# Reordering the first batch of a fused attention and feed-forward kernel: earlier loads of the second batch, and score bursts of 384 columns

## The chip, the cores and the metric

The kernel runs on one core of a Trainium2 chip. The metric is the device time of one execution in microseconds (us). The kernel before took 431.75 us (median of three runs, 431.38 to 431.86).

## What is computed

The reference is grouped-query attention followed by a feed-forward layer with a squared ReLU, over 8 batches (b0 to b7) of 384 tokens:

```python
scores = scale * np.matmul(q, k.transpose(0, 1, 3, 2))   # q: 8 x 16 heads x 384 x 64, k and v: 8 x 4 kv heads, each serving 4 heads
attn = exp(scores - max);  attn = attn / sum(attn)
x = matmul(attn, v).transpose(0, 2, 1, 3).reshape(3072, 1024)
h = np.maximum(x @ w_in, 0.0)        # w_in: 1024 x 2048
out = (h * h) @ w_out                # w_out: 2048 x 1024
```

Inputs and output are f32; the kernel computes in bf16 with f32 accumulation and leaves out the subtraction of the maximum.

## The kernel before, in words

**Work of a batch.** The 384 tokens are three blocks of 128. A batch has four kv groups (g0 to g3) of four heads, and 12 units: one kv group with one block of keys. The scores of a unit are 128 keys by 1536 columns (4 heads x 384 queries), held as two halves x=0,1 of 768 columns (two heads each, stacked on partitions 0-63 and 64-127 of `qT`). ScalarE (ACT) takes `exp` of them from PSUM into `expT`. A "pair" c (two per kv group) is the product of the exponentials with the values, 18 matmuls with 65 columns in function `av`; its last column is the softmax sum, by which VectorE (DVE) divides (`rinv`, `o_sb`). The result is turned into `xT` (in b0 on TensorE, `turn_o_pe`; later by a transposing DMA, `turn_o_dma`). The feed-forward part of a batch is 128 "up" matmuls (line 426: 16 column blocks of 8) and 96 "down" matmuls (line 471: six outputs of 16), with relu on DVE (434), square on ACT (436), output copies on DVE (480) and stores on SP (483).

**Keys and queries must be turned** before scores: keys are doubled into `k_dup`, then keys and queries are turned into `kT` and `qT`. For b0 and b1 TensorE does it (`turn_k_pe`, three transposes; `turn_q_pe`, six) with a DVE copy after each; from b2 on SP issues transposing DMAs (lines 266 and 272).

**Order of the work.** The kernel is written as a list. `Recorder.add` appends an operation to its engine's list, with the tiles that it reads and writes, and works out a modelled end from a `cost`; `emit` gives each engine its list in that order with the semaphore waits that follow. So the order on every engine is fixed when the program is built. TensorE's order is chosen by the loop at lines 575 to 675: at each step it collects what could come next (a turn, a pair, a turn of the output, a score burst, a piece of the feed-forward) with the modelled time at which its inputs are there, and takes among those that are ready the one with the lowest priority number: score bursts of b0 are 0, turns 1, pairs 2, output turns 3, later score bursts 4, feed-forward 5.

**Scores of b0** come in small bursts (`burst_small`, list `smalls`), of 1024 values per partition each: a whole unit's columns 0 to 511, and after each second unit the columns 512 to 767 of two units together. That is 18 bursts and 18 `exp` instructions at line 337. A burst takes two of PSUM banks 0 to 3 alternately; turns and pairs share banks 4 and 5 while b0's bursts last, and the feed-forward has banks 6 and 7. Batches b1 to b7 use `burst_two` (lines 347 and 357): two units, six banks, 3072 values per partition.

**Loads.** The queue of GpSimd (POOL) carries nearly all loads, with a cast from f32. After b0's own loads and three key copies, it issues w_in pieces 0 to 2 (512 KB each), then keys (192 KB), queries (two of 384 KB) and values of b1, then w_in pieces 3 to 7, then the key copy `k_dup` and value copy `v_aug` of b1, four pieces of w_out (1024 KB each), and then keys, queries and values of b2. The first keys and queries of b0 come uncast over the SP and ACT queues: `q_f32` in one transfer, cast by DVE (columns 0 to 511 of 768) and by ACT (columns 512 to 767). The queries of g0 are turned in two steps: tiles 0 to 3, then tiles 4 and 5.

Of the kernel before, what the change touches and what calls it, by code (L numbers as in the profile page):

```python
# [133 lines left out]
def bass_gqa_attention__then__ffn_squared_relu_kernel(  # L134
# [72 lines left out]
    def first_loads():  # L207

        def keys(eng, g0, g1):
            R.add(eng, lambda e: e.dma_start(  # L210
                k_f32[:, g0 * NJ:g1 * NJ, :].rearrange("p (g j) d -> p g (j d)", j=NJ),
                k[0, g0:g1].rearrange("g (p j) d -> p g (j d)", j=NJ)),
                writes=[("k_f32", g) for g in range(g0, g1)], dma=f"kf{g0}", cost=0.4 * (g1 - g0), issue=0.4)

        keys("sync", 0, 1)
        R.add("scalar", lambda e: e.dma_start(
            q_f32[:, :, :], q[0, 0:4].rearrange("h (p j) d -> p h (j d)", j=NJ)),
            writes=["q_f32"], dma="qf", cost=1.3, issue=0.4)
        keys("scalar", 1, HKV)
# [8 lines left out]
    def load_q(b, h0, h1):  # L228
        st = b % NST
        R.add("gpsimd", lambda g: g.dma_start(  # L230
            q_st[st][:, h0:h1, :],
            q[b, h0:h1].rearrange("h (p j) d -> p h (j d)", j=NJ)),
            writes=[("q_st", st, h // 4, x) for h in range(h0, h1, 4) for x in range(2)], dma=f"q{st}_{h0}",
            cost=0.33 * (h1 - h0), issue=0.8)
# [36 lines left out]
    def turn_q_dma(b, half):  # L271
        R.add("sync", lambda e: e.dma_start_transpose(
            out=qT[b % 2][:, 12 * half:12 * half + 12, :],
            in_=q_st[b % NST][:, 8 * half:8 * half + 8, :].rearrange("p h e -> p (h e)")),
            reads=[("q_st", b % NST, 2 * half + i, x) for i in range(2) for x in range(2)],
            writes=[("qT", b % 2, 2 * half + i, x) for i in range(2) for x in range(2)], dma=f"turn_q{half}", cost=2.5)

# [15 lines left out]
    def turn_q_pe(b, g, banks, t0=0, t1=6):  # L293
        i = pick(banks)
        pt = bank(i).bitcast(bf16)
        src = q_st[b % NST][:, 4 * g:4 * g + 4, :].rearrange("p h e -> p (h e)")
        parts = [h for h in range(2) if t0 < (4, 6)[h] and t1 > (0, 4)[h]]

        def tr(pe):
            for t in range(t0, t1):  # L300
                m = pe.matmul(pt[:, (t - t0) * 128:(t - t0 + 1) * 128], src[:, t * 128:(t + 1) * 128], ident[:],  # L301
                              is_transpose=True)
            return m

        R.add("tensor", tr, reads=[("q_st", b % NST, g, h) for h in parts] + ["ident"], writes=[("bank", i)],
              cost=0.06 * (t1 - t0))
        dst = qT[b % 2][:, 6 * g + t0:6 * g + t1, :].rearrange("p n c -> p (n c)")
        R.add("vector", lambda e: e.tensor_copy(dst, pt[:, 0:(t1 - t0) * 128]),  # L308
              reads=[("bank", i)], writes=[("qT", b % 2, g, h) for h in parts], cost=0.07 + 0.068 * (t1 - t0))


    def score_reads(b, u, parts=(0, 1)):
        g = u // NJ
        return [("kT", b % 2, g)] + [("qT", b % 2, g, h) for h in parts]

# [4 lines left out]
    def burst_small(b, pieces, base):  # L320

        wide = 512 // len(pieces)

        def sc(pe):
            for n, (u, c0) in enumerate(pieces):
                for x in range(2):
                    m = pe.matmul(ps[:, base + x, n * wide:(n + 1) * wide],  # L327
                                  kT[b % 2][64 * x:64 * x + 64, u, :], q_cols(b, u // NJ, x, c0, c0 + wide))
            return m

        keys = [("bank", base), ("bank", base + 1)]
        R.add("tensor", sc, reads=[r for u, c0 in pieces for r in score_reads(b, u, (c0 // 512,))], writes=keys,
              cost=0.22 + 0.19)
        n, c0 = (b * NU + pieces[0][0]) % NEX, pieces[0][1]
        src = ps[:, base:base + 2, :].rearrange("p x (k c) -> p x k c", k=len(pieces))
        dst = expT[:, n:n + len(pieces), :, c0:c0 + wide].rearrange("p k x c -> p x k c")
        R.add("scalar", lambda e: e.activation(dst, src, AF.Exp, scale=0.125),  # L337
              reads=keys, writes=[("expT", (n + m) % NEX, c0 // 512) for m in range(len(pieces))], cost=0.92)

    def burst_two(b, u):  # L340

        def sc(pe):
            for k0, cols in ((0, ((0, 512), (512, 768))), (1, ((0, 256), (256, 768)))):
# [13 lines left out]
        R.add("scalar", lambda e: e.activation(dst, src, AF.Exp, scale=0.125),  # L357
              reads=keys, writes=[("expT", (n + m) % NEX, h) for m in range(2) for h in range(2)], cost=2.63)

    def av_reads(b, g):  # L360
        return [("expT", (b * NU + g * NJ + j) % NEX, h) for j in range(NJ) for h in range(2)] + [("v_aug", b % 2), ("v_one", b % 2)]

    def av(b, c, banks):
# [11 lines left out]

        R.add("tensor", lambda pe: mm(pe, 6 * s2), reads=av_reads(b, g), writes=[("bank", i)], cost=0.285)
        yield
        R.add("tensor", lambda pe: mm(pe, 6 * s2 + 3), reads=av_reads(b, g), writes=[("bank", i)], cost=0.285)
        r = (b * 8 + c) % 2
# [125 lines left out]
    aug_v(0, "gpsimd")  # L505
    for i in range(3):
        load_w_in(i)
    load_k(1)
    load_q(1, 0, 8)
    load_q(1, 8, 16)  # L510
    load_v(1)
    for i in range(3, 8):
        load_w_in(i)
    dup_k(1, "gpsimd")
    aug_v(1, "gpsimd")
# [7 lines left out]
    def warm_up(pe):  # L523
        for _ in range(14):
# [6 lines left out]
    q_from = q_f32.ap().rearrange("p h e -> p (h e)")  # L531
    R.add("vector", lambda e: e.tensor_copy(q_to[:, 0:512], q_from[:, 0:512]),
          reads=["q_f32"], writes=[("q_st", 0, 0, 0)], cost=0.6)
    R.add("scalar", lambda e: e.copy(q_to[:, 512:768], q_from[:, 512:768]),
          reads=["q_f32"], writes=[("q_st", 0, 0, 1)], cost=0.4)

# [3 lines left out]
    for u in range(NU):  # L540
        smalls.append([(u, 0)])
        if u % 2 == 1:
            smalls.append([(u - 1, 512), (u, 512)])
    turn_q = [(0, 0, "k"), (0, 0, "a"), (0, 0, "c")]
# [4 lines left out]
    turned_g = set()  # L549
    units, halves, pairs, turned, up_done = 0, set(), 0, 1, -1  # L550
    x_done = {b: 0 for b in range(B)}
# [16 lines left out]
    def open_bank(banks):  # L568
        return min(R.when(writes=[("bank", i)]) for i in banks)
# [5 lines left out]
    while av_q or av_open or sc_q or o_q or f_head is not None:  # L575
# [3 lines left out]
        if loaded + 1 < B and turned >= loaded and not turn_q:  # L579
# [5 lines left out]
            load_v(loaded)  # L585
        if not chores and queued < loaded and units >= queued * NU and pairs >= queued * 8:
            queued += 1
            prepare(queued)
# [5 lines left out]
        if turn_q:  # L594
            b, g, w = turn_q[0]
            src = [("k_dup", b, g)] if w == "k" else [("q_st", b, g, h) for h in range(2) if w != "ac"[1 - h]]
            cand.append((max(R.when(reads=src), open_bank(spare)), 1, "turn"))
        if av_open is not None:
            cand.append((now, 2, "av2"))
        elif av_q:  # L600
            b, c = av_q[0]
            if units >= b * NU + (c // 2 + 1) * NJ and up_done >= b - NXT:
                cand.append((max(R.when(reads=av_reads(b, c // 2)), open_bank(spare)), 2, "av"))
        if o_q:
            cand.append((max(R.when(reads=o_q[0][2]), open_bank(spare)), 3, "o"))
        if sc_q:
            b, u = sc_q[0]
            if b == 0:
                top = max(p[0] for p in smalls[u])
                ok = all((0, p[0] // NJ, p[1] // 512) in turned_g for p in smalls[u])  # L610
                ok = ok and pairs // 2 * NJ + NEX >= top + 1
                reads = [r for p in smalls[u] for r in score_reads(0, p[0], (p[1] // 512,))]
                t = max(R.when(reads=reads), R.when(writes=[("bank", 2 * (u % 2) + i) for i in range(2)]))
                if ok:
                    cand.append((t, 0, "sc"))
            else:
                ok = ((b, (u + 1) // NJ, 1) in turned_g) if b == 1 else turned >= b
                t = max(R.when(reads=score_reads(b, u) + score_reads(b, u + 1)),
# [17 lines left out]
        if what[2] == "turn":  # L636
            b, g, w = turn_q.pop(0)
            if w == "k":
                turn_k_pe(b, g, spare)
            else:  # L640
                turn_q_pe(b, g, spare, *dict(q=(0, 6), a=(0, 4), c=(4, 6))[w])
            turned_g |= {(b, g, h) for h in range(2) if w in ("q", "ac"[h])}
        elif what[2] == "av":
# [17 lines left out]
        elif what[2] == "sc":  # L661
            b, u = sc_q.pop(0)
            if b == 0:
                burst_small(0, smalls[u], 2 * (u % 2))
                halves |= {(p[0], p[1] // 512) for p in smalls[u]}
                while (units, 0) in halves and (units, 1) in halves:
                    units += 1
            else:
                burst_two(b, u)
                units += 2  # L670
        else:
# [34 lines left out]
```

The softmax here doesn't subtract the row's maximum and nothing guards it: scores larger than these inputs give would overflow.

## Time and profile before

| | us |
|---|---|
| median of three runs | 431.75 |
| span of the profiled execution | 430.6 |
| TensorE busy | 421.8 |
| ScalarE busy | 194.0 |
| VectorE busy | 158.9 |
| GpSimd busy | 55.6 |
| up matmuls, 1024 at line 426 | 174.5 |
| down matmuls at line 471 | 167.7 |
| `exp` of b0, 18 at line 337 | 16.9 |
| `exp` of b1 to b7, 42 at line 357 | 114.5 |

A row of the timeline gives the start, the length of a merged run of equal instructions, the engine, the line, output and inputs, the shape and the count; a bracket at its end gives the idle time of the engine before it and what ended that idle time. Matmul ends are modelled, so rows that overlap by a few tenths are one uninterrupted stream.

### The profile page before, as it was taken

Reading aid. Unit: us, or ns where it says so; the run is one execution under the profiler, and the core shown is the slowest. Engines: PE = TensorE matmul, PEld = TensorE weight load, DVE = VectorE, ACT = ScalarE, POOL = GpSimd, SP = SyncE. Lnnn points to the kernel's source line nnn. Section 1 sums busy time; section 2 is a strip of 40 time slices with the busy share of each in tenths; the row PEclk is TensorE's granted clock in tenths of the full one; section 3 lists DMA queues with packets and bytes.
Section 4 is the critical chain, followed back from the end, with each engine's and each line's share of the span. In section 5 each row is a group of like instructions: output and inputs, shape, how many; then the busy total and the mean of one; then the engine's idle time right before and its main releaser. Section 6 shows DMA issues by size and latency. Waiting matters only on the chain.

```text
span 430.6 us, 7790 instructions
## 1 busy us (share of the span) xinstructions
PE 421.8 (98%) x3428; PEld 231.6 (54%) x3454; DVE 158.9 (37%) x335; ACT 194.0 (45%) x190; POOL 55.6 (13%) x68
## 2 busy tenths in 40 slices
PE   8899999999999999999999999999999999999997
PEld 4465555465454655546555455645564455446544
DVE  3474422254233543225433243533342144224412
ACT  4937750557545576455773549540241034003300
POOL 7752002404040031004000000000000000000000
DMA  8999999999596189299553230042101100110012
GB/s 147 182 195 202 190 198 215 200 191 138 105 175 156 37 137 131 85 144 166 60 103 94 70 85 0 2 106 69 49 2 49 73 26 1 50 73 26 1 63 85
DMA packets 95331, 43.90 MB, mean 102 GB/s; under 512 B 75712, under 2 KB 89280, under 8 KB 95296
## 3 DMA queue, kind: packets, MB, share of 16 engines
q0 software_dynamic: 36544, 17.44, 32.3%
q1 hardware_dynamic: 57824, 25.27, 26.4%
q10 hardware_dynamic: 928, 0.69, 0.5%
q8 instruction: 27, 0.44, 0.4%
q14 instruction: 8, 0.07, 0.1%
HBM read 35.65 MB, written 12.58 MB: 112 GB/s over the span
## 4 chain that ended last, share of the span: by engine, by line
PE 92%; ACT 3%; DMA 2%; DVE 1%; SPq 1%; issue 1%
PE ps L426 39%; PE ps L471 37%; PE ps L347 7%; PE ps L372 7%; ACT expT L337 3%; DMA qT<-q_st 1%; DMA q_f<-in_q_dram 1%; PE ps L301 1%; SPq L266 1%; DVE o_sb L387 1%; PE ps L327 0%; PE ps L285 0%; DVE qT L308 0%; DVE y_sb L480 0%; DVE rinv L381 0%
## 5 line engine op out<-in xcount | busy, mean ns | idle before, releaser
L426 PE MATMUL ps<-xT,w_in_sb 128*128 128x384 bf16 x1024 | 174.5, 326 | 0.0
L471 PE MATMUL ps<-w_out_sb,h2T 128*128 128x512 bf16 (+2 forms) x758 | 167.7, 375 | 1.7 <-issue 0.5
L357 ACT ACTIVATE expT<-ps 128x3072 bf16<-128x3072 f32 x42 | 114.5, 2725 | 70.9 <-PE ps L347 70.0
L426 PEld LDWEIGHTS ps<-xT,w_in_sb 128*128 128x128 bf16 x1024 | 97.0, 98 | 69.3 <-issue 6.2
L436 ACT ACTIVATE h2T<-hr 128x384 bf16<-128x384 f32 x128 | 64.4, 520 | 138.0 <-DVE hr L434 137.8
L471 PEld LDWEIGHTS ps<-w_out_sb,h2T 128*128 128x128 bf16 x784 | 73.6, 98 | 87.9 <-issue 6.0
L434 DVE TENSOR_SCALAR hr<-ps 128x384 f32<-128x384 f32 x128 | 71.2, 557 | 103.9 <-PE ps L426 103.9
L480 DVE COPY y_sb<-ps 128x512 f32<-128x512 f32 (+2 forms) x49 | 33.3, 681 | 130.7 <-PE ps L471 130.7
L372 PEld LDWEIGHTS ps<-v_aug,expT 128*128 128x128 bf16 x1152 | 39.8, 97 | 6.7 <-issue 0.7
L372 PE MATMUL ps<-v_aug,expT 128*128 128x65 bf16 x1152 | 41.4, 193 | 0.3 <-ACT expT L337 0.3
L387 DVE TENSOR_TENSOR o_sb<-ps,rinv 128x384 bf16<-128x384 f32 x64 | 35.6, 557 | 2.4 <-DVE rinv L381 0.2
L347 PE MATMUL ps<-qT,kT 64*128 64x512 bf16 (+1 forms) x336 | 34.6, 325 | 0.5 <-DMA qT<-q_st 0.5
L347 PEld LDWEIGHTS ps<-qT,kT 64*128 64x128 bf16 x336 | 13.0, 94 | 21.2 <-DVE o_sb L387 4.9
L381 DVE RECIPROCAL rinv<-ps 128x6 f32<-128x6 f32 x64 | 12.1, 190 | 25.5 <-PE ps L372 25.5
L337 ACT ACTIVATE expT<-ps 128x1024 bf16<-128x1024 f32 x18 | 16.9, 1070 | 2.4 <-PE ps L327 2.2
L262 POOL COPY v_aug<-v_st 128x768 bf16<-128x768 bf16 x8 | 6.6, 830 | 83.7 <-PE ps L372 67.8
L230 POOL DMA_DIRECT2D q_st<-in_q_dram x17 | 15.0, 896 | 0.9 <-POOLq L691 0.8
L257 POOL COPY k_dup<-k_st 128x1536 bf16<-128x1536 bf16 x7 | 10.3, 1469 | 37.1 <-DMA k_st<-in_k_dram 37.1
L202 POOL DMA_DIRECT2D k_st<-in_k_dram x7 | 5.3, 757 | 39.9 <-DMA qT<-q_st 39.9
L327 PE MATMUL ps<-qT,kT 64*128 64x512 bf16 (+1 forms) x48 | 7.5, 360 | 1.8 <-ACT expT L337 1.3
L240 POOL DMA_DIRECT2D w_in_sb<-in_moe_w_in_dram x8 | 7.1, 935 | 0.0
L223 POOL DMA_DIRECT2D v_st<-in_v_dram x8 | 6.3, 788 | 0.1
(26 smaller groups left out, 42.8 us busy)
## 6 DMA issues: line engine op xcount, KB each, us to landing
out_dram<-y_sb SPq DMA_DIRECT2D x47, 256.0 KB, 2.0
q_st<-in_q_dram POOLq DMA_DIRECT2D x14, 384.0 KB, 8.9
w_in_sb<-in_moe_w_in_dram POOLq DMA_DIRECT2D x8, 512.0 KB, 16.1
w_out_sb<-in_moe_w_out_dram POOLq DMA_DIRECT2D x4, 1024.0 KB, 26.4
v_st<-in_v_dram POOLq DMA_DIRECT2D x8, 192.0 KB, 9.8
k_st<-in_k_dram POOLq DMA_DIRECT2D x7, 192.0 KB, 3.9
q_st<-in_q_dram POOLq DMA_DIRECT2D x3, 192.0 KB, 5.7
xT<-o_sb SPq DMA_TRANSPOSE x28, 2.8
```

The lines of the kernel that those rows point to most:

```text
L230: R.add("gpsimd", lambda g: g.dma_start(q_st[st][:, h0:h1, :], q[b, h0:h1].rearrange("h (p j) d -> p h (j d)", j=NJ)), writes=[("q_st", st ...
L337: R.add("scalar", lambda e: e.activation(dst, src, AF.Exp, scale=0.125), reads=keys, writes=[("expT", (n + m) % NEX, c0 // 512) for m in r ...
L347: m = pe.matmul(flat[:, k0 * HC + c0:k0 * HC + c1], kT[b % 2][64 * x:64 * x + 64, u + k0, :], q_cols(b, (u + k0) // NJ, x, c0, c1))
L357: R.add("scalar", lambda e: e.activation(dst, src, AF.Exp, scale=0.125), reads=keys, writes=[("expT", (n + m) % NEX, h) for m in range(2) ...
L372: m = pe.matmul(po[:, f - 6 * s2, 0:D + 1], w, v_aug[b % 2][:, g * NJ + j, 0:D + 1], start=(j == 0), stop=(j == NJ - 1))
L381: R.add("vector", lambda e: e.reciprocal(rinv[r].ap().unsqueeze(2), po[:, :, D:D + 1]), reads=[("bank", i)], writes=[("rinv", r)], cost=0.13)
L387: R.add("vector", lambda e: e.tensor_tensor(dst, srcv, rbv, ALU.mult), reads=[("bank", i), ("rinv", r)], writes=[("o_sb", o, s2)], cost=0.48)
L426: m = pe.matmul(bank(i)[:, 0:S], w_in_sb[:, kc, c * 128:(c + 1) * 128], xT[b % NXT][:, kc, :], start=(kc == 0), stop=(kc == NKC - 1))
L434: R.add("vector", lambda e: e.tensor_scalar_max(hr[r][:, :], bank(i)[:, 0:S], 0.0), reads=[("bank", i)], writes=[("hr", r)], cost=0.48)
L436: R.add("scalar", lambda e: e.activation(h2T[b % 2][:, c, :], hr[r][:, :], AF.Square), reads=[("hr", r)], writes=[("h2T", b % 2, c)], cost ...
L471: m = pe.matmul(bank(i)[:, 0:n], h2T[b % 2][:, c, i3 * 128:(i3 + 1) * 128], w_out_sb[:, c, c0:c1], start=(c == 0), stop=(c == NFC - 1))
L480: R.add("vector", lambda e: e.tensor_copy(ysl, bank(i)[:, 0:n]), reads=[("bank", i)], writes=[("y", yb)], cost=0.08 + n / 960)
```

## The change

It has five parts.

1. **Loads of b1.** On POOL's queue the keys and both query halves of b1 stand before all of w_in; then follow w_in pieces 0 and 1, the values of b1, the copy `k_dup` of b1, and w_in pieces 2 to 7. The rest of the queue is as before.
2. **First queries of b0.** `q_f32` comes in two transfers of two heads each. DVE casts both halves (384 columns each); ACT's copy is gone. The turn of g0's queries is split into tiles 0 to 2 and 3 to 5.
3. **Bursts of the first and last kv group.** For g0 and g3 of b0 a burst is one unit with 384 columns of each half (768 values per partition), first the columns 0 to 383 of all three units, then the columns 384 to 767. In the two groups between them the bursts stay as they were, except in the first unit of g1 and the last of g2, which are cut in two bursts of 384 columns. In all there are 16 bursts of 768 values and 6 of 1024.
4. **Dependencies by tile of 128 columns.** `qT` and `expT` were tracked in two parts per unit, now in six tiles. A pair now depends on its own three tiles of the group's three units, not on the whole units.
5. **Turns of b1** get priority number 4.5 (before: 1), so they go behind pairs and output turns, ahead of the feed-forward.

The order that follows on TensorE differs in b0, in b1's turns and in the feed-forward of b0 up to the first score burst of b2; behind that it is the same as before. Up to the first burst of b1, 12 up matmuls are issued (before: 28); the other 16 come later in the feed-forward of b0. The last pair of b1 that precedes the first burst of b2 has 68 down matmuls between it and that burst (before: 52).

```diff
-        R.add("scalar", lambda e: e.dma_start(
-            q_f32[:, :, :], q[0, 0:4].rearrange("h (p j) d -> p h (j d)", j=NJ)),
-            writes=["q_f32"], dma="qf", cost=1.3, issue=0.4)
+        for n in range(2):
+            R.add("scalar", lambda e, n=n: e.dma_start(
+                q_f32[:, 2 * n:2 * n + 2, :], q[0, 2 * n:2 * n + 2].rearrange("h (p j) d -> p h (j d)", j=NJ)),
+                writes=[("q_f32", n)], dma=f"qf{n}", cost=0.8, issue=0.4)
...
-    for i in range(3):
-        load_w_in(i)
     load_k(1)
     load_q(1, 0, 8)
     load_q(1, 8, 16)
+    for i in range(2):
+        load_w_in(i)
     load_v(1)
-    for i in range(3, 8):
+    dup_k(1, "gpsimd")
+    for i in range(2, 8):
         load_w_in(i)
-    dup_k(1, "gpsimd")
     aug_v(1, "gpsimd")
...
-    R.add("vector", lambda e: e.tensor_copy(q_to[:, 0:512], q_from[:, 0:512]),
-          reads=["q_f32"], writes=[("q_st", 0, 0, 0)], cost=0.6)
-    R.add("scalar", lambda e: e.copy(q_to[:, 512:768], q_from[:, 512:768]),
-          reads=["q_f32"], writes=[("q_st", 0, 0, 1)], cost=0.4)
+    R.add("vector", lambda e: e.tensor_copy(q_to[:, 0:384], q_from[:, 0:384]),
+          reads=[("q_f32", 0)], writes=[("q_st", 0, 0, 0)], cost=0.45)
+    R.add("vector", lambda e: e.tensor_copy(q_to[:, 384:768], q_from[:, 384:768]),
+          reads=[("q_f32", 1)], writes=[("q_st", 0, 0, 1)], cost=0.45)
...
     for u in range(NU):
-        smalls.append([(u, 0)])
-        if u % 2 == 1:
-            smalls.append([(u - 1, 512), (u, 512)])
+        if NJ < u < NU - NJ - 1:
+            smalls.append([(u, 0, 512)])
+            if u % 2 == 1:
+                smalls.append([(u - 1, 512, 256), (u, 512, 256)])
+        elif u in (NJ, NU - NJ - 1):
+            smalls += [[(u, 384 * n, 384)] for n in range(2)]
+        elif u % NJ == 0:
+            smalls += [[(u + j, 384 * n, 384)] for n in range(2) for j in range(NJ)]
...
-            cand.append((max(R.when(reads=src), open_bank(spare)), 1, "turn"))
+            cand.append((max(R.when(reads=src), open_bank(spare)), 3.5 * b + 1, "turn"))
...
-            if units >= b * NU + (c // 2 + 1) * NJ and up_done >= b - NXT:
-                cand.append((max(R.when(reads=av_reads(b, c // 2)), open_bank(spare)), 2, "av"))
+            needs = {(b, c // 2 * NJ + j, 3 * (c % 2) + t) for j in range(NJ) for t in range(3)}
+            if needs <= scored and up_done >= b - NXT:
+                cand.append((max(R.when(reads=av_reads(b, c)), open_bank(spare)), 2, "av"))
...
-                turn_q_pe(b, g, spare, *dict(q=(0, 6), a=(0, 4), c=(4, 6))[w])
+                turn_q_pe(b, g, spare, *dict(q=(0, 6), a=(0, 3), c=(3, 6))[w])
```

## The prediction

> **What bounds the kernel now.** I read the page first, then the chain of waits, then TensorE's timeline with ScalarE's and SP's beside it.
>
> ```profile
> PE 421.8 (98%) x3428; PEld 231.6 (54%) x3454; DVE 158.9 (37%) x335; ACT 194.0 (45%) x190; POOL 55.6 (13%) x68
> ...
> PE 92%; ACT 3%; DMA 2%; DVE 1%; SPq 1%; issue 1%
> ```
>
> TensorE is busy for 98% of the span, and the chain that ended last is 92% TensorE. The change removes no matmul outside b0's scores, so it can only win idle time of TensorE. The chain names two places where something else led: ACT's `exp` of b0 (3%, line 337) and a DMA (2%). The timeline shows them.
>
> ```profile
> 4.68 0.41 ACT L534 CAST q_st<-q_f 128x256 bf16<-128x256 f32 x1 [1.62 <-DMA q_f<-in_q_dram]
> 6.94 3.08 ACT L337 ACTIVATE expT<-ps 128x1024 bf16<-128x1024 f32 x3 [1.85 <-PE ps L327]
> 10.33 14.10 ACT L337 ACTIVATE expT<-ps 128x1024 bf16<-128x1024 f32 x15 [0.30 <-PE ps L327]
> ```
>
> ACT works from 6.94 to 24.43 almost without a gap: b0 is paced by ACT, and TensorE fills in.
>
> ```profile
> 24.48 1.30 PE L372 MATMUL ps<-v_aug,expT 128*128 128x65 bf16 x36 [0.30 <-ACT expT L337]
> 25.62 0.33 PE L405 MATMUL ps<-ident,o_sb 128*128 128x128 bf16 x3
> 26.11 0.34 PE L405 MATMUL ps<-ident,o_sb 128*128 128x128 bf16 x3 [0.15 <-DVE o_sb L387]
> 26.80 0.34 PE L405 MATMUL ps<-ident,o_sb 128*128 128x128 bf16 x3 [0.35 <-DVE o_sb L387]
> ```
>
> After the last `exp` come two pairs (36 matmuls), their division and three output turns; TensorE waits for DVE. From 27.07 it is dense, b1's turns run from 28.38 to 30.40, and b1's first burst starts at 32.45. One wait follows:
>
> ```profile
> 66.25 11.17 PE L471 MATMUL ps<-w_out_sb,h2T 128*128 128x512 bf16 x50
> 77.87 0.82 PE L347 MATMUL ps<-qT,kT 64*128 64x512 bf16 x8 [0.45 <-DMA qT<-q_st]
> ```
>
> TensorE is there at 77.42 and b2's turned queries land at about 77.8. SP's queue shows why:
>
> ```profile
> 67.18 1.22 SPq L392 DMA_TRANSPOSE xT<-o_sb  x1
> 69.54 0.33 SPq L483 DMA_DIRECT2D out_dram<-y_sb  x1
> 69.92 3.54 SPq L266 DMA_TRANSPOSE kT<-k_dup  x1
> 73.50 3.86 SPq L272 DMA_TRANSPOSE qT<-q_st  x2
> ```
>
> The key turn stands behind b0's third output store, which TensorE paces, and behind an output turn. The transfers share the DMA engines with the loads: 190 to 215 GB/s in slices 3 to 9 of the page.
>
> **What the Trainium skill says.** "ScalarE: Activation LUTs", What ACT_TABLE_LOAD costs: an ACTIVATE takes 186 ns + 0.833 ns per element, and back-to-back ones overlap by about 93 ns. That gives 946 ns per 1024 values; the trace agrees (14.10/15 = 940 ns). "TensorE: Matmul & The Clock Gate", What's actually happening: TensorE runs at half clock until some 3.4 us of activity. The trace fits: six transposes take 0.82 to 0.85 us up to 8.4 us, and 0.51 from 10.6 on (the page's clock figure doesn't show it). "DMA: Bandwidth & Descriptors", Queues, rings and completion order: a DMA engine takes its queues in turn, packet by packet. The trace agrees: from 64 to 68 us both the load queue (78.8%) and the other (57.7%) have packets under way, and an output turn issued then lands after 7.1 us (median of all: 2.8).
>
> **The change part by part.** Sum against the span, 430.6; the runs lie 1.15 above it (431.75), and I keep that distance.
>
> (a) *First queries.* All four heads land at 3.93 us after issue (0.73), at 4.66. 384 KB in two parts: by the nearest row (96 KB of keys, 2.8 us) the first half lands between 3.5 and 4.2, the second by 4.7. DVE's casts: keys 3.53 to 4.08, first half 0.33 (512 columns took 0.43), second 4.67 to 5.0. The key copy then starts at 5.0 (before 5.03), the first query copy ends at 5.7, and the burst starts at 5.75 (before 6.29). It has 384 columns rather than 512, at half clock 0.11 less, so the first `exp` starts at about 6.26 (before 6.94): **0.7 earlier**. One more DMA issue on ACT (0.46) stands ahead of the other keys; they land at 6.6 behind the queries on the same queue, so I take 0 (bounds 0 and 0.46 late). The table load (1.28) has no wait and fits before 6.26. ACT's copy (0.41) was beside DVE's and is worth nothing itself.
>
> (b) *Bursts.* 18 x 0.946 = 17.03 becomes 6 x 0.946 + 16 x 0.733 = 17.40: **0.37 more** of ACT. TensorE's side: a score burst of 512 columns costs 0.32 in the timeline, one of 384 about 0.28; four more bursts hide under ACT.
>
> (c) *Start of b0.* The third burst stands behind the key turn of g1, which waits for POOL's copy (7.27 before), then 0.5 of transposes and 0.5 of burst: the third `exp` starts at 8.25 while the second ended at 7.85, a gap of 0.4. The six transposes of g1's queries (0.85) give another 0.25. Then 0.73 per `exp` is met: eight are done at 13.1. The remaining 6 x 0.946 + 8 x 0.733 = 11.54 end at **24.65** (before 24.43). Between two bursts stands at most one pair (0.67), and the bursts have two slots, so I take no further gap; bounds: 0.6 fewer (no early gaps), 0.5 more.
>
> (d) *End of b0.* Only one pair is left after the last `exp`, 18 matmuls. Under the last two `exp`s go two output turns, one query and two key turns of b1. Then, from 24.75: pair at 24.95, 0.65; three query and two key turns of b1, 3 x 0.34 + 2 x 0.17 = 1.36; DVE's division of the last pair (0.20 + 0.48, behind four turn copies) ends at 26.7, so the last output turn goes at 26.95; 12 up matmuls from 27.1, 12 x 0.163 = 1.96; burst of b1 at **29.06**. 16 up matmuls (2.61) are owed, so this compares with 31.67, against 32.45: **0.78 gained**. Before, DVE's waits left TensorE idle here; now b1's turns stand there.
>
> (e) *Loads.* The quickest w_in piece landed 5.9 us after issue; I take it for piece 0, issued at 8.96. It now has 960 KB ahead, at 195 GB/s 5 us: about 20, needed at 27.1. Piece 1 at 22.7, needed at 30.5. Piece 2 takes the place that b1's values had (27.4), needed at 33; later pieces stand as before. POOL's key copy of b1 waits for its keys, but behind the issue of w_in and values at about 14, when they have landed: queued behind it are w_in 2 to 7, with 2.2 MB under way. Cost 0. The value copy, which waits for b1's values, holds w_out and b2's loads; those values land some 3 us earlier (27.39 before). Cost 0.
>
> (f) *The wait at 77.87.* The total of loads ahead of b2's queries is the same. TensorE arrives at 77.42 - 0.78 = 76.64. The third store comes 0.78 earlier too (68.8), after `k_dup` (66.13 + 1.47 = 67.6), and the output turn of the last pair now lies 16 down matmuls (3.56 us) further ahead, so it is out of the key turn's way. I let the turn land 1.1 earlier, 76.7: the wait shrinks from 0.45 to about 0.1. Bounds: 0 earlier (gain lost) to 1.3.
>
> Sum: 77.87 becomes 76.8, **1.07 gained**. The rest of TensorE's order is unchanged. 430.6 - 1.07 = 429.5 in the span, 430.7 in the runs.
>
> **The rivals.**
>
> *The DMA keeps the gain (same).* The key turn took 3.54 us to issue at 69.92 and loads went on until 74.12, when b2's values had landed. If that, not the third store, sets the landing at 77.8, TensorE comes sooner and waits 1.2 instead of 0.45: 431.6, reaching 431.0 if a part is kept. For it: the DMA engines are full throughout. Against it: the output turn leaves that queue 3.5 us sooner.
>
> *ACT stays dense (faster).* Without the gaps in (c), ACT ends at 6.26 + 17.40 = 23.7; 0.95 more is gained: 429.8, if the key turn follows its store (`k_dup`, ready at 67.6, allows it). For it: those gaps rest on half-clock durations; against it: POOL's copy at 7.2 is waited for in any case.
>
> *Bursts of 0.73 starve ACT (slower).* TensorE executes in order, and a pair (0.67) plus a burst (0.28) is longer than one short `exp`. If half clock lasts a window of 3.4 us longer, or the DVE copies behind banks 4 and 5 come late, each of the 16 short ones waits 0.15 to 0.2: 2.4 to 3.2 lost, against 0.78 gained and 0.45 of wait to absorb it. 432.9; it decides from 0.13 us a burst.
>
> That the change doesn't do what it says is excluded: the built order shows it.
>
> **How the numbers follow.** Forecast 0.45 (430.0 to 431.2), DMA keeps the gain 0.28, ACT dense 0.14, starved 0.13. A measurement tells 0.2%, 0.86 us, from no change, so faster means under 430.9: two thirds of the forecast, all of the dense case and a tenth of the second give 0.47; slower, over 432.6, is most of the starved case and errors unnamed, 0.12; the rest, 0.41, is the same. The range leaves out the far starved case and the end of the dense one: 429.6 to 432.0.
>
> **What would show it.** Right: the first `exp` at 6.3, the last ending at 24.4 to 25, one pair after it, b1's first burst near 29.1, the first burst of b2 near 76.8 with under 0.3 of wait. Wrong: gaps over 0.2 between `exp`s after 13 us; w_in as releaser of line 428; the burst of b2 still at 77.8 with a wait over 1.

## The result and the profile after

The changed kernel took **436.75 us** (median of four runs, 433.83 to 437.45) against 431.73 of the kernel before, run beside it: ratio of the means 1.0105, 95% interval 1.0059 to 1.0151. Measured a second time (run 5 below) it took 434.68 us (four runs, 433.97 to 434.93) against 431.85: ratio 1.0062 (1.0047 to 1.0077). It is slower, by 0.6 to 1%; 430.7 was forecast. The profile below is of the 437.45 run, the slowest, with a span of 435.6 us; each kernel below was profiled in one execution, the changed one in two.

The page's engine totals and its shares of the chain that ended last:

```profile
PE 425.7 (98%) x3454; PEld 232.4 (53%) x3454; DVE 159.4 (37%) x336; ACT 194.2 (45%) x193; POOL 55.3 (13%) x68
...
PE 93%; DMA 3%; ACT 1%; SPq 1%; POOL 0%; ACTq 0%; DVE 0%; issue 0%
```

Of the chain, ACT fell from 3% to 1%, as meant; DMA rose from 2% to 3%. TensorE is busy 3.9 us longer; part of that is matmul records missing from the trace before (3428 for 3454 weight loads), part is work that ran slower. ScalarE's timeline (start, length, engine, line, operation; idle time before in the bracket) shows the first loss:

```profile
6.06 1.51 ACT L338 ACTIVATE expT<-ps 128x768 bf16<-128x768 f32 x2 [2.51 <-PE ps L328]
9.61 2.55 ACT L338 ACTIVATE expT<-ps 128x768 bf16<-128x768 f32 x3 [2.04 <-PE ps L328]
12.54 2.40 ACT L338 ACTIVATE expT<-ps 128x768 bf16<-128x768 f32 x3 [0.38 <-PE ps L328]
15.13 11.44 ACT L338 ACTIVATE expT<-ps 128x1024 bf16<-128x1024 f32 x14 [0.18 <-PE ps L328]
```

The first `exp` comes at 6.06 (before 6.94), but after two of them ACT waits 2.04 us, then 0.38. Only from 15.13 on is it dense; the last `exp` ends at 26.57 (before 24.43). TensorE's timeline says what was missing:

```profile
8.96 0.34 PE L286 MATMUL ps<-ident,k_dup 128*128 128x128 bf16 x3 [2.62 <-POOL k_dup L258]
9.23 0.34 PE L328 MATMUL ps<-qT,kT 64*128 64x384 bf16 x2
...
9.94 0.50 PE L328 MATMUL ps<-qT,kT 64*128 64x384 bf16 x2
...
11.25 0.82 PE L302 MATMUL ps<-ident,q_st 128*128 128x128 bf16 x6
...
13.76 0.34 PE L328 MATMUL ps<-qT,kT 64*128 64x384 bf16 x2
...
81.28 1.15 PE L349 MATMUL ps<-qT,kT 64*128 64x512 bf16 x8 [2.32 <-DMA qT<-q_st]
82.35 3.22 PE L473 MATMUL ps<-w_out_sb,h2T 128*128 128x512 bf16 x8
```

In the front it waits 2.62 us for the keys of kv group 1, and a microsecond after that wait bursts take 0.50 in place of 0.34, six turns 0.82 in place of 0.51: half clock, until 13.3 (the clock that the profile gives as granted to TensorE is 0.50 there, from 10 to 12 us). The copy that it waits for is POOL's. POOL's timeline, first of the kernel before, then of the changed one:

```profile
6.71 1.41 POOL L257 CAST k_dup<-k_f 128x384 bf16<-128x384 f32 x3 [1.30 <-DMA k_f<-in_k_dram]
...
8.96 2.64 POOL L240 DMA_DIRECT2D w_in_sb<-in_moe_w_in_dram  x3
```

```profile
8.40 1.40 POOL L258 CAST k_dup<-k_f 128x384 bf16<-128x384 f32 x3 [3.15 <-DMA k_f<-in_k_dram]
...
10.52 0.75 POOL L202 DMA_DIRECT2D k_st<-in_k_dram  x1
```

The keys land 1.7 us later. POOL stands still for them, and the loads queued behind them are issued from 10.52 on, not from 8.96. This delay comes back 70 us later. The chain of waits of the changed kernel (start, length, what):

```profile
64.28 6.06 PE ps L473 x28
70.34 1.48 POOL k_dup L258
...
71.83 2.57 SPq L267
...
74.44 6.79 DMA qT<-q_st
...
81.28 1.15 PE ps L349 x8
```

The key copy of b2, at 66.13 in the kernel before, comes at 70.34; SP's key turn and first query turn follow it, and the query turn lands at 81.2. (The chain puts the wait ahead of the copy down to a matmul that ended at the same moment; the load of b2's keys landed then too, at 70.27.) But the late copy by itself costs little. SP's key turn stands behind b0's third output store as well, issued at 71.08, and SP's waits from 60 to 84 us (total, times, longest) give the copy only the last 0.4:

```profile
SPq L485 <- DVE y_sb L482: 7.7, 3, 3.5
SPq L394 <- DVE o_sb L389: 1.9, 1, 1.9
SPq L267 <- POOL k_dup L258: 0.4, 1, 0.4
```

The greater part is the flight of the turns. The key turn lands 8.1 us after its issue (before 6.4) and the query turn 6.8 us (before 4.3), beside loads that end late: b2's values land at 79.0, before at 74.1. The last two rows of TensorE's timeline above show what that costs: it waits 2.32 us, and the eight down matmuls behind the burst take 3.22 us (before 1.90): half clock again (granted 0.50 from 82 to 84 us). From the first burst of b2 to the end of the span pass 352.7 us in the kernel before and in every profile below without that second half clock (351.9 in runs 4, 8 and 10, whose built order differs around that burst), and 354.3 or 354.4 in those with it. So the end follows from this burst, and each run below is read by it.

| profile | key copies of g1 | last `exp` ends | b1's first burst | TensorE at b2's burst | wait there | span |
|---|---|---|---|---|---|---|
| before | 6.71 | 24.43 | 32.45 | 77.42 | 0.45 | 430.6 |
| changed | 8.40 | 26.57 | 30.89 | 78.96 | 2.32, half clock | 435.6 |
| changed, again | 8.35 | 27.30 | 31.63 | 79.69 | 0.70 | 433.1 |

(Ahead of b1's first burst stand 28 up matmuls in the kernel before and 12 in the changed one, so that column compares only rows of one order.)

### The profile page after: what moved, and what is told of

Its sections match the earlier page's. It is cut to its first block, busy times and chain, and to the rows that moved or that the text cites. A ratio compares the mean times of both kernels' runs of the same rounds, so it can differ in the third digit from the quotient of the medians.

```text
span 435.6 us, 7822 instructions
## 1 busy us (share of the span) xinstructions
PE 425.7 (98%) x3454; PEld 232.4 (53%) x3454; DVE 159.4 (37%) x336; ACT 194.2 (45%) x193; POOL 55.3 (13%) x68
## 4 chain that ended last, share of the span: by engine, by line
PE 93%; DMA 3%; ACT 1%; SPq 1%; POOL 0%; ACTq 0%; DVE 0%; issue 0%
PE ps L428 39%; PE ps L473 37%; PE ps L374 8%; PE ps L349 7%; DMA qT<-q_st 2%; DMA k_f<-in_k_dram 2%; ACT expT L338 1%; PE ps L328 1%; PE ps L302 1%; SPq L267 1%; POOL k_dup L258 0%; PE ps L286 0%; ACTq L217 0%; PE ps L407 0%; DVE hr L436 0%
## 5 line engine op out<-in xcount | busy, mean ns | idle before, releaser
L473 PE MATMUL ps<-w_out_sb,h2T 128*128 128x512 bf16 (+2 forms) x784 | 173.3, 377 | 0.0
L473 PEld LDWEIGHTS ps<-w_out_sb,h2T 128*128 128x128 bf16 x784 | 74.1, 98 | 89.4 <-issue 8.0
L349 PE MATMUL ps<-qT,kT 64*128 64x512 bf16 (+1 forms) x336 | 34.9, 327 | 2.3 <-DMA qT<-q_st 2.3
L338 ACT ACTIVATE expT<-ps 128x768 bf16<-128x768 f32 (+1 forms) x22 | 17.7, 873 | 5.3 <-PE ps L328 5.1
L258 POOL COPY k_dup<-k_st 128x1536 bf16<-128x1536 bf16 x7 | 10.3, 1475 | 40.2 <-PE ps L473 36.6
L328 PE MATMUL ps<-qT,kT 64*128 64x384 bf16 (+2 forms) x48 | 8.5, 374 | 0.6 <-ACT expT L338 0.6
```

What stands on the lines that cost most here:

```text
L328: mm = pe.matmul(ps[:, base + x, m * wide:(m + 1) * wide], kT[b % 2][64 * x:64 * x + 64, u, :], q_cols(b, u // NJ, x, c0, c0 + wide))
L349: m = pe.matmul(flat[:, k0 * HC + c0:k0 * HC + c1], kT[b % 2][64 * x:64 * x + 64, u + k0, :], q_cols(b, (u + k0) // NJ, x, c0, c1))
L473: m = pe.matmul(bank(i)[:, 0:n], h2T[b % 2][:, c, i3 * 128:(i3 + 1) * 128], w_out_sb[:, c, c0:c1], start=(c == 0), stop=(c == NFC - 1))
```

## The experiments

Theory A: the second query transfer makes the keys of g1 to g3 late; TensorE idles in the front of b0 (theory H: and falls to half clock), and POOL, held by the keys, starts the loads late, which is the wait at b2. The first four kernels undo or isolate parts. Ratios are of means, against the kernel before run beside each.

**1. One query transfer in the changed kernel.** The order on every engine is otherwise that of the changed kernel.

```diff
-        for n in range(2):
-            R.add("scalar", lambda e, n=n: e.dma_start(
-                q_f32[:, 2 * n:2 * n + 2, :], q[0, 2 * n:2 * n + 2]...
+        both = R.add("scalar", lambda e: e.dma_start(
+            q_f32[:, :, :], q[0, 0:4].rearrange("h (p j) d -> p h (j d)", j=NJ)),
```

> The changed kernel with the first queries of b0 in one transfer again; the order of the work on every engine is that of the changed kernel. Theory A (late keys: the second query transfer puts the keys of g1 to g3 behind it, their late landing holds GpSimd's queue, all later loads start late, and b2's first burst waits for them): the keys land at about 6.7 us, the load of b1's keys is issued at about 9.0 (10.5 in the changed kernel), b2's first burst starts at 77 to 78 (81.3) and the time is 430.5 to 431.8. Theory B (the new order of the loads does it) and theory C (short bursts starve ScalarE): still 434 or more, with b2's burst at 80 or later.

Measured: 432.98 us (20 runs, 431.43 to 436.21), ratio 1.0020 (1.0004 to 1.0037). Most of the loss goes, and no gain appears: the figure lies above theory A's and below that of B and C. Keys are copied from 6.52, b1's first burst is at 30.04, a microsecond later than the prediction had for the whole change. The profile is that of the slowest run, and there the burst of b2 waits 1.92 us and half clock follows; four of the 20 runs lie at 435.1 to 436.2, the other 16 at 431.4 to 433.5.

**2. Only the two transfers, in the kernel before.**

```diff
+        for n in range(2):
+            R.add("scalar", lambda e, n=n: e.dma_start(
+                q_f32[:, 2 * n:2 * n + 2, :], ...
```

> The kernel before with the first queries in two transfers and nothing else; the order on every engine is that of the kernel before. Theory A: the keys of g1 to g3 land after 8 us instead of 6.7, the first w_in load is issued at about 10.5 instead of 9.0, b2's first burst waits 1.5 to 3 us instead of 0.45, and the time is 433 to 436. Theories B and C: within 0.5 us of the kernel before.

Measured: 434.18 us (20 runs), ratio 1.0051 (1.0040 to 1.0061). The issues of DMAs by ScalarE and SP before 2.6 us, with KB and the time from issue to landing; first of the kernel before, then of this one:

```profile
q_f<-in_q_dram ACTq DMA_DIRECT2D x1, 384.0 KB, 3.9
k_f<-in_k_dram ACTq DMA_DIRECT2D x1, 288.0 KB, 5.4
```

```profile
q_f<-in_q_dram ACTq DMA_DIRECT2D x2, 192.0 KB, 3.2
k_f<-in_k_dram ACTq DMA_DIRECT2D x1, 288.0 KB, 6.1
```

The same 288 KB of keys, issued one DMA issue later, also need 0.7 us longer (1.2 in the changed kernel, 6.6); they are copied from 7.89. TensorE waits 1.80 us for them, b1's first burst is 1.49 us later than before (33.94), and there is no wait at b2 at all. The loss is in the front alone; the wait that was expected at b2 did not come.

**3. Keys on SP's queue, ahead of the second query half, in the changed kernel.**

```diff
-        keys("scalar", 1, HKV)
+        keys("sync", 1, HKV)
```

> The changed kernel with the keys of g1 to g3 issued from SP's queue, ahead of the second half of the queries; every other order is kept. Theory A: the keys land before 6.7 us, and the time is 430.0 to 431.5, the forecast's gain or most of it. Theories B and C: still 434 or more.

Measured: 433.88 us (16 runs), ratio 1.0037 (1.0026 to 1.0048), between the figures of the theories. Keys are copied from 5.30 and the wait at b2 is gone, but the front lost by another way. VectorE's timeline:

```profile
3.91 0.36 DVE L536 CAST q_st<-q_f 128x384 bf16<-128x384 f32 x1
5.33 1.61 DVE L538 CAST q_st<-q_f 128x384 bf16<-128x384 f32 x1 [1.06 <-DMA q_f<-in_q_dram]
```

The second half lands later, and its cast, the same operation, takes 1.61 us in place of 0.36: it ran beside POOL's three casts (5.30 to 6.72). "GPSIMD Engine Reference", 1. Specifications, of the Trainium skill says that POOL shares its memory interfaces with VectorE and contends with VectorE's two-port modes; the stretch agrees, though no run shows the mode. This run therefore does not isolate the keys.

**4. The old order of the loads in the changed kernel.**

```diff
+    for i in range(3):
+        load_w_in(i)
     load_k(1)
...
-    for i in range(2):
-        load_w_in(i)
```

> The changed kernel with w_in pieces 0 to 2 ahead of b1's loads, as before (TensorE's order then follows: some up matmuls come back between b0's bursts). Theory A: the late keys are still there, so b2's burst still waits over 1.5 us and the time stays at 433.5 to 437. Theory B: back to 431 to 432. Theory C: 433 or more, but without the wait at b2.

Measured: 434.31 us (12 runs), ratio 1.0047 (1.0035 to 1.0058). Keys late (7.82), TensorE waits 1.98 for them, no wait at b2, the key copy of b2 at 67.04. As written, that is the outcome of theory C, and theory A missed its wait; runs 8 and 10 below speak against C. Late keys alone, then, make no wait at b2 (2 and 4). In these profiles it comes with the new order of loads, and with how late that starts: none with a first load at 8.98 (run 3), 1.92 us at 9.35 (the profile of run 1), 0.70 to 2.74 us at 10.3 to 10.5 (the changed kernel and run 9).

**5. The changed kernel once more**, beside the next three.

> The changed kernel once more, in the same call as the three beside it. If its loss is fixed by the program (keys late, key copies hold GpSimd, loads of b2 late), the median is again 435.5 to 437.5 and the wait ahead of the first burst of b2 is 1.5 to 3 us; if the first figure was an accident of four executions, it comes at 432.5 to 434, with that wait under 0.7.

Measured: 434.68 us. The front repeats (third row of the table above) and so do the keys at 8.35; at b2 TensorE waits only 0.70, and its clock stays:

```profile
80.39 0.82 PE L349 MATMUL ps<-qT,kT 64*128 64x512 bf16 x8 [0.70 <-DMA qT<-q_st]
81.15 1.90 PE L473 MATMUL ps<-w_out_sb,h2T 128*128 128x512 bf16 x8
```

Neither expectation held whole: the loss in the front is fixed, the second varies, and that is most of the difference between the two medians.

**6. Loads of b1's keys and queries ahead of POOL's key copies.**

```diff
+    early = [i for i, o in enumerate(R.ops) if o["dma"] in ("k1", "q1_0", "q1_8")][:3]
...
+    order = rest[:rest.index(copy)] + early + rest[rest.index(copy):]
```

> The changed kernel with the loads of b1's keys and queries issued on GpSimd ahead of its key copies of b0, where it idles until the keys land; all else in place. Theory A (the late keys hold GpSimd, which starts all loads 1.6 us late, and that is the wait of 2.3 us and the half clock at the first burst of b2): the first of these loads is issued by 5.5 us in place of 10.5, the last keys of b2 are copied by 67.5 in place of 70.3, the wait at the first burst of b2 falls under 0.7 us, and the time falls by 2.5 to 4 us to 432.5 to 434, the front's 1.8 us remaining. Rival (the loads' transfers are slow by themselves, whenever issued): wait still over 1.5 us, time within 1 us of the changed kernel. Second rival (the early loads share the queues' engines with the keys, which land another 1 us or more late): key copies begin at 9.3 us or later and the time is 435 or more.

Measured: 433.57 us, ratio 1.0038 (1.0023 to 1.0053), as theory A had it. The first of these loads is issued at 5.22, the key copy of b2 comes at 64.89, the wait at b2 is gone (burst at 78.33). Keys were not later for it (copied from 7.83). The time is 1.1 us under that of run 5, measured beside it, so the fall of 2.5 to 4 us is met only against the first median of the changed kernel. What made the wait go can be read from the turns of b2:

| profile | key copy done | key turn issued | lands after | query turn issued | lands after | b2's values landed | wait at b2 |
|---|---|---|---|---|---|---|---|
| before | 67.60 | 69.92 | 6.4 | 73.50 | 4.3 | 74.1 | 0.45 |
| changed | 71.80 | 71.83 | 8.1 | 74.44 | 6.8 | 79.0 | 2.32 |
| changed, again (5) | 71.06 | 72.20 | 6.9 | 74.54 | 5.8 | 77.6 | 0.70 |
| run 1 | 70.35 | 70.60 | 8.0 | 73.60 | 6.4 | 77.6 | 1.92 |
| run 6 | 66.36 | 70.90 | 4.7 | 72.88 | 4.3 | 72.6 | none |

In run 6 the key turn is issued only 0.9 us earlier than in the changed kernel, as it still stands behind the third output store; but its flight is 3.4 us shorter and the query turn's 2.5. In runs 1 and 5 the copy was done before the key turn's turn came, and TensorE waited all the same. So the late loads reach TensorE mainly through the flights of the turns, which are long where the loads end late. (In run 9 the late copy did hold the key turn, for 1.4 us: the third store was issued at 69.69, the copy was done at 71.42.) That the turns and the loads share the DMA engines fits every row, but no run moved the turns alone to show it.

**7. The same with one query transfer.** Both edits above.

> As the run before, and the queries of b0 in one transfer as in the kernel before. Theory A: keys land by 6.5, no wait over 0.5 us at the first burst of b2, and 430 to 431.7 us, level with the kernel before or up to 0.4% under it. Rival (half-clock bursts in the front and the new order of the loads cost what they cost): 432.5 to 433.5, as with one transfer and loads in the changed place.

Measured: 433.13 us, ratio 1.0027 (1.0015 to 1.0039): the rival's figure. No wait at b2, but the edit spoiled its own front: POOL was still issuing loads until 7.7, so it copied the keys from 7.72 without having waited for them. Half clock lasts to 13.3, and b1's first burst is at 30.99.

**8. One query transfer and old load order**, which leaves of the change the bursts pair by pair, the two query casts on VectorE and the place of the turns.

> The changed kernel with queries of b0 in one transfer and the loads of w_in ahead of the keys of b1 as in the kernel before: of the change only the bursts pair by pair of the first and last group of b0 and the early turns remain. Theory A (the split alone makes the keys late): keys land by 6.5, no wait at the first burst of b2, and 431 to 432.5 us, within 0.2% of the kernel before. Rival (384-column bursts cost by themselves, at half clock in the front): 433.5 to 434.5, as with the split and the old loads.

Measured: 432.53 us (20 runs, 431.03 to 433.53), ratio 1.0011 (1.0001 to 1.0020), just over the top of theory A's range. Keys from 5.58, no wait at b2, and half clock from 7.5 to 10.7: the last `exp` ends at 25.06. That is one execution; five of the 20 took 431.0 to 431.3 us, as fast as the next version of this kernel (run 10).

**9. Warm-up matmuls in the wait for the late keys.** The changed kernel, ten more 128x256 matmuls on TensorE ahead of g1's key turn.

```diff
+            if (b, g, w) == (0, 1, "k"):
+                def filler(pe):
+                    for _ in range(10):
+                        m = pe.matmul(bank(7)[:, 0:256], warm[:, 0:128], warm[:, :])
```

> The changed kernel with ten warm-up matmuls (128x256, into a bank nothing reads) on TensorE ahead of the key turn of kv group 1, in the idle time in which it waits for the late keys; all else in the same order. Theory H (the gap leaves TensorE at half clock until 13.4 us, and in that window the short bursts and turns, 0.50 and 0.82 us in place of 0.34 and 0.51, starve ScalarE): turns and bursts come at full speed from 10 us on, the gap of 0.38 us among the exps after 12 us goes, the first burst of b1 stands at 29.5 to 30.2 us (30.9 and 31.6 in the two profiles of the changed kernel), and the time is 0.7 to 1.5 us lower, 433.2 to 435. Rival (only the waiting for the keys counts): first burst of b1 within 0.3 us of 30.9, time 434.5 to 436.7.

Measured: 436.04 us, ratio 1.0087 (1.0068 to 1.0106). TensorE's timeline of this kernel:

```profile
6.11 1.26 PE L649 MATMUL ps<-warm 128*128 128x256 bf16 x10
8.72 0.34 PE L286 MATMUL ps<-ident,k_dup 128*128 128x128 bf16 x3 [1.34 <-POOL k_dup L258]
...
9.26 0.51 PE L302 MATMUL ps<-ident,q_st 128*128 128x128 bf16 x6
...
29.50 0.82 PE L349 MATMUL ps<-qT,kT 64*128 64x512 bf16 x8
...
80.31 0.88 PE L349 MATMUL ps<-qT,kT 64*128 64x512 bf16 x8 [2.74 <-DMA qT<-q_st]
```

In the front theory H holds: turns and bursts stay at full speed though the keys are as late as before (8.16), the gaps of 0.38 are gone, b1's first burst is 1.39 us earlier than in the changed kernel. The time missed its figure and lies in the rival's range, though the rival's mark, the burst at 30.9, is not there: at b2 TensorE now waits 2.74 us. What the front won, the loads took back.

**10. Warm-up matmuls in the version of 8**: four ahead of the first query turn, one ahead of the second, two after g1's key turn.

```diff
+            count = {(0, 0, "a"): 4, (0, 0, "c"): 1}.get((b, g, w), 0)
+            if count:
+                filler(count)
```

> The version with bursts pair by pair, one query transfer and the old order of the loads, with seven warm-up matmuls in TensorE's three gaps between 4.5 and 7.5 us (four ahead of the first query turn, one ahead of the second, two after the key turn of group 1). Theory H: turns and bursts at full speed from 8 to 9 us on (10.7 without), the last exp of b0 ends by 24.5 (25.06 without), and 430.8 to 431.8 us, 0.5 to 1 under the version without and level with the kernel before or up to 0.2% under it. Rival (ScalarE's start, not the clock, sets the front of b0, or the clock does not answer to short fillers): within 0.3 us of the version without, 432.2 to 432.8.

Measured: **431.36 us** (21 runs, 430.65 to 432.61), ratio 0.9988 (0.9982 to 0.9995): under the kernel before, by half a microsecond. ScalarE's timeline now has a single row for b0:

```profile
6.72 17.42 ACT L340 ACTIVATE expT<-ps 128x768 bf16<-128x768 f32 x22 [3.66 <-PE ps L330]
```

All 22 `exp` without a gap; the 17.42 us are the 17.40 of step (b).

**11. Warm-up matmuls in the kernel before**, two and one ahead of the query turns of g0.

> The kernel before with three warm-up matmuls in TensorE's gap ahead of the query turns of group 0 (two ahead of the first, one ahead of the second). Theory H: the kernel before pays for half clock only until 10 us and its exps wait there 0.30 us in all, so 431.4 to 431.8 us, nothing that can be told from the kernel before. Rival (every gap of the front is dear): 430.5 to 431.2.

Measured: 432.01 us (13 runs), ratio 1.0001 (0.9992 to 1.0009). The last `exp` ends at 23.75 and b1's first burst is at 31.78, both 0.7 us earlier; but the wait at b2 grows from 0.45 to 1.04, and the burst stands at 77.78 (77.87 before). In the old load order a gain of the front alone is kept by the DMA.

**12. Both repairs (6 and 9) in the changed kernel.**

> The changed kernel with both repairs: the ten warm-up matmuls in the wait for the late keys, and the loads of b1's keys and queries issued on GpSimd ahead of its key copies. If the loss is these two together (half clock in the front, and loads behind the late keys), the repairs add up: first burst of b1 at 29.0 to 29.7 us, TensorE reaches the first burst of b2 by 77.7 and waits there under 0.4 us, and the time is within 0.2% of the kernel before (431.0 to 432.7 us). Rival (the front's gain always comes back at the first burst of b2, since the loads end no earlier than in the kernel before): first burst of b2 at 78.3 us or later with a wait over 0.7, and 432.8 us or more.

Measured: 431.92 us (13 runs, 431.61 to 432.22), ratio 1.0000 (0.9992 to 1.0008). TensorE's timeline:

```profile
29.14 0.82 PE L350 MATMUL ps<-qT,kT 64*128 64x512 bf16 x8
...
77.14 0.82 PE L350 MATMUL ps<-qT,kT 64*128 64x512 bf16 x8
```

The two repairs add up, and with them the changed order stands where it was forecast (29.06 and 76.8), with no wait at b2. Its span of 429.8 is 0.8 under that of the profile before, but the medians are equal; the kernel before was profiled in a run of 432.37, above its median. Not all is repaired: g1's key turn still waits 1.27 us for late keys.

## Why the prediction was wrong

By the first profile the burst of b2 came at 81.28, forecast 76.8, and half clock cost another 1.6: together the 6.1 us between the forecast span of 429.5 and 435.6.

- **(a), first part: right.** First `exp` at 6.06 (forecast 6.26), with two DVE casts of 0.36.
- **(a), "they land at 6.6 behind the queries on the same queue, so I take 0": the step that failed.** They landed at 8.35, 1.7 us late; the outer bound had been 0.46. The added issue was counted, but not that behind it the keys travel beside POOL's cast loads, whose issue ends at 5.25. Run 2 shows the loss with nothing else changed, 0.5%. That sharing is the cause fits the 0.7 us longer flight, but no run took POOL's loads away to show it.
- **(c): failed with it.** The third `exp` came at 9.61, not 8.25; gaps of 2.04, 0.38 and 0.18 us in place of 0.4 and 0.25. Last `exp` at 26.57 for 24.65: 1.9 of the 4.5 us. Run 9 splits this: with nearly the same late keys but full clock it ends at 25.17, so 1.2 to 1.4 of it is half clock, the rest waiting. (The sum had a slip too: 8.25 + 6 x 0.733 + 0.25 gives 12.9 for the eighth `exp`, not 13.1.)
- **(b) and (d): right.** ACT's work came to 17.42 in run 10. From the last `exp` to b1's first burst passed 4.32 us (forecast 4.41).
- **After (d), a term left out.** From b1's first burst to the arrival at b2's passed 48.07 us, forecast 47.58. In it is a wait of 0.33 for DVE's relu, four up matmuls behind the burst.
- **(e), "Cost 0", and (f): failed.** POOL's copies wait for b0's late keys, and the first load behind them is issued 1.56 us late. (f) was right that the key turn stands behind the third store and the copy hardly holds it (0.4 us). But the store came at 71.08 and not at 68.8, and (f) let the turns land 1.1 us earlier; their flights took 8.1 and 6.8 us in place of 6.4 and 4.3. The wait at b2 became 2.32, not 0.1: 2.2 of the 4.5 us, and the half clock behind it 1.6 more. Run 6 shows that the late loads make it: with three of them ahead of POOL's wait, it vanishes.
- **How 1.56 us at the start became 4.2 us at b2's key copy** the bytes show in part. At 60 us the load queue had moved 9.83 MB in the kernel before and 9.40 in the changed one; at the 0.18 MB per us that it moved from 20 to 60 us, the 0.43 MB are an estimated 2.3 us. From there to the landing of b2's keys (10.85 and 10.89 MB) it was slower, 0.145 MB per us for 0.169, while SP's turns and stores moved 0.50 MB for 0.13. Why 1.56 us had grown to 2.3 by 60 us stays open; under the old order the copy came only 0.9 us late (67.04, run 4).
- **From the span to the runs: a wrong distance.** The prediction set the span of the profiled run, 430.6, against the median of other runs, 431.75, and kept 1.15. The profiled run itself took 432.37, 1.77 above its span (run 12: 1.84). The forecast span of 429.5 thus stood for some 431.3 us, not 430.7, and for a gain of 0.4 us on the median.
- **The rivals.** "DMA keeps the gain" named the right place, the burst of b2 behind its turned queries; run 11 shows that rival in the kernel before. Its reason, loads still under way beside the turns, is what the flights show; its price assumed loads as early as before. "Starve ACT" had half clock lasting longer, but for all 16 short bursts: from 15.13 on, and in run 10 from the start, bursts of 768 values did not starve ACT.

Put together, runs 6, 9 and 12 account for the loss: it was two waits and the half clock behind each, not the new bursts. Without the wait at b2 and without half clock the change is worth nothing that can be measured (run 12, where the wait for the late keys is left); with one query transfer, the old loads and a warm TensorE it is worth 0.12% (run 10).

## What to carry to other kernels

One more DMA issue ahead of a transfer is not priced by its issue time: look at what other queue starts in that time, and who stands still in order behind the landing. An in-order queue such as POOL's turns a late input into late loads, and these are paid far from the cause, so follow each queue behind a new wait to its last customer, and cost transfers beside it by flights measured beside busy loads. In the first microseconds and behind each wait of 2 us, cost TensorE's work at half clock as well. Filling such gaps with matmuls that nothing reads pays only where what comes next can use it: it did in runs 10 and 12, and won nothing in runs 9 and 11. And take the distance from span to time from the profiled run itself.

## What the runs showed of the hardware

- **Waits shorter than the stated window put TensorE back to half clock.** "TensorE: Matmul & The Clock Gate", What's actually happening, of the Trainium skill gives at least one idle window, some 3.4 us, free-running. Here waits of 1.92 (run 1), 2.32 (changed) and 2.74 us (run 9) were followed by half clock, with eight down matmuls at 3.57, 3.22 and 3.48 us; waits of 0.70 (run 5) and 1.04 us (run 11) were not (1.90). The measurement decides: about 2 us was enough here.
- **A warm-up can fail by gaps of under a microsecond.** In the one profile of run 8 TensorE falls to half clock from 7.5 to 10.7 us behind gaps of 0.93, 0.18 and 0.47 us; with seven matmuls in those gaps (run 10) it does not. In the kernel before gaps of 0.52 and 0.31 us follow the 14 warm-up matmuls, and six turns take 0.82 to 0.85 us up to 8.4; with three matmuls there (run 11) they take 0.50 from 6.80 on. So the 3.4 us of activity, which the prediction found to fit, did not do by themselves: in the kernel before TensorE had worked for 3.6 us without a gap by 4.64.
- **The same program can start warm or cold.** In two executions of the changed kernel the three transposes at 4.01 us take 0.53 and 0.35 us.
- **The granted clock does not show every slow stretch.** Behind the waits it reads 0.50; in the kernel before, where six turns take 0.82 to 0.85 us, it reads 1.00. The lengths of equal instructions are the surer sign.
- **A turn's flight depends on what else is under way**: the key turn of b2 took 4.7 us (run 6) to 8.1 us (changed).
- **VectorE's casts stretch beside POOL's**: 0.36 to 1.61 us (run 3).
